# A planner that follows all DMA transfers as a fluid, without hand-set nudges, and with a new order of loads

## The chip, the cores and the metric

The kernel runs on one core of one Trainium2 chip. The metric is device time in microseconds (us), lower is better. "Span" is the time from the first to the last instruction in one profiled execution; the device time of the same execution is some 1.8 us longer. Runs that are compared were made on the same chip in one sitting, the kernel before among them each time. Slow executions are left out of every ratio; a single execution has no known state.

## The reference

Windowed attention with a few global keys and a linear distance bias, then a two-layer block with the activation h - tanh(h):

```python
# q, k, v: (4 batches, 8 heads, 768 positions, 64), n_global = 8, n_local = 96
scores = scale * np.matmul(q, k.transpose(0, 1, 3, 2))
...
keep = is_global | is_local
bias = -slopes[:, None, None] * dist[None, :, :]
scores = np.where(keep, scores + bias, -1e9)
a = softmax(scores)                                  # cut: max, exp, sum written out
attn_out = np.matmul(a, v)

x = attn_out.transpose(0, 2, 1, 3).reshape(B * S, H * D)   # (3072, 512)
h = x @ w_in                                         # (512, 2048)
g = h - np.tanh(h)
return g @ w_out                                     # (2048, 512)
```

## The kernel before

The 3072 rows are 24 query tiles of 128. Each tile goes: load q, k, v (GpSimd); transpose q and k (on TensorE for tiles 0 to 5, by a DMA from SyncE from tile 6 on); scores (TensorE); exponential (ScalarE); mask (DVE); attention times v (TensorE); normalize (DVE); transpose x (TensorE, from tile 9 on a DMA from SyncE); the first product `m1` (TensorE); tanh (ScalarE); h - tanh(h) (DVE, called `g`); the second product `m2` (TensorE); eviction (ScalarE or DVE); store (issued by ScalarE). The operations that matter below:

```python
def a_DT(u):                                  # transpose of q and k, one DMA
    qk[u] = kpool.tile([P, 2, NP, P], BF16, name="qk")
    nc.sync.dma_start_transpose(out=..., in_=kq.pop(u)...)          # cut

def m1_th(g, f0):                             # ScalarE, PSUM -> "th", 3 buffers
    nc.scalar.activation(h_view(ths[g, f0], g, m), h_view(hs[g, f0], g, m), AF.Tanh, bias=0.0, scale=1.0)

def m1_g(g, f0):                              # DVE, frees the PSUM bank of m1
    nc.vector.tensor_tensor(out=gs[b][:, f0 : f0 + m, o : o + n], in0=h_view(hs.pop((g, f0)), g, m),
                            in1=h_view(ths.pop((g, f0)), g, m), op=ALU.subtract)

def store(u, part):
    lo, hi = parts(u)[part]
    eng = nc.sync if u == NU - 1 else nc.scalar
    eng.dma_start(out=out[SEQ[u] * P : (SEQ[u] + 1) * P, lo:hi], in_=ots[u][:, lo:hi])
```

The order on each engine isn't written by hand. A planner simulates the engines when the program is built: again and again it takes the operation that can start first, with its own estimate of durations, buffers, PSUM banks and DMA landings. The instructions are then emitted in the order of planned start. An engine executes them strictly in that order.

```python
op(("st", u, part), SP if u == NU - 1 else ACT, ..., lambda ...: store(u, part), after=[("ev", u, part)],
   give=["ot"] if part == len(parts(u)) - 1 else [], dma=T_ST)
...
NUDGE = { ('AV', 21): -0.3, ('E', 12, 1): 0.3, ... ('m2', 2, 1): 1.0, ... }   # 58 entries; cut
...
ring = {SP: [0.0, []], POOL: [5.8, []]}       # two DMA queues; ScalarE's stores count as SP
...
    via = POOL if o["eng"] is POOL else SP
    if o["dma"] and len(ring[via][1]) >= 8:   # at most eight in flight
        t = max(t, sorted(ring[via][1])[-8])
    ...
    c = (round(t + NUDGE.get(key, 0.0), 3), o["pri"], n)      # the least c goes next
...
order, model_end = plan()
with tc.manual_schedule(engines={PE, ACT, DVE, POOL, SP}):
    ...
    for t, key in with_warm(order):
        ops[key]["fn"]()
```

The softmax here doesn't subtract the row's maximum and nothing guards it: scores larger than these inputs give would overflow.

## Time and profile before

| | before |
|---|---|
| device time, median of the first 3 runs (lowest to highest) | 214.13 us (213.65 to 215.67) |
| span of the profiled execution | 212.3 us |
| TensorE busy | 203.8 us, 96% |
| granted TensorE clock | 1.0 in the mean |
| stalls of TensorE after the start | 1.21 us at 55.6 us, 0.73 us at 71.8 us |

The prediction below shows the lines of the profile and builds an account from them, with the terms "work ahead" and "lag".

How to read the lines: a timeline row has start, duration, engine, source line, operation, tiles, shapes, count, and in square brackets the idle time before it with what ended that. "ACTq" and "SPq" are the DMA issues of ScalarE and SyncE. A row of a waits view has the engine that waited, what it waited for, the total in us, the number of times, and the longest.

### The profile page before, as it was taken

What the parts mean: (1) busy time and instruction counts of PE and PEld (TensorE: products, weight loads), DVE (VectorE), ACT (ScalarE), POOL (GpSimd) and SP (SyncE); (2) the same over time, 40 slices, a digit from 0 to 9 for tenths busy, and PEclk for the clock granted to TensorE, in tenths of its full rate; (3) what the DMA queues carried; (4) which work ended last, traced back from release to release, by engine and by line L of the source; (5) the groups of instructions that cost most, each with busy time, mean ns of one, the idle gap of its engine ahead of it and who ended that gap; (6) DMA issues with size and microseconds to landing.
All of it is one profiled execution on the core that took longest, in us unless ns stands there. A gap on an engine that the chain in (4) does not pass through costs nothing.

```text
span 212.3 us, 5296 instructions
## 1 busy us (share of the span) xinstructions
PE 203.8 (96%) x2172; PEld 145.4 (68%) x2198; DVE 132.1 (62%) x269; ACT 120.4 (57%) x184; POOL 71.9 (34%) x92
## 2 busy tenths in 40 slices
PE   7899999999799899999999999999999999999994
PEld 2679995984466767577677578757755786666754
DVE  6579796656475777385667487757655594343611
ACT  4777865553446786487358465667545773444410
POOL 8995676667344365345342700000000000000000
PEclk9999999999999999999999999999999999999999
DMA  5999999999999999999999999212362220110112
GB/s 181 182 189 177 180 203 180 187 157 167 159 158 186 151 137 181 144 181 184 153 169 164 165 142 193 50 74 53 99 112 90 77 49 0 52 51 16 37 49 100
DMA packets 106073, 27.49 MB, mean 129 GB/s; under 512 B 94656, under 2 KB 103104, under 8 KB 106048
## 3 DMA queue, kind: packets, MB, share of 16 engines
q0 software_dynamic: 74048, 13.11, 84.9%
q1 hardware_dynamic: 28144, 7.48, 26.6%
q10 hardware_dynamic: 3856, 6.56, 9.7%
q8 instruction: 17, 0.28, 0.6%
q14 instruction: 8, 0.07, 0.1%
HBM read 27.26 MB, written 6.29 MB: 158 GB/s over the span
## 4 chain that ended last, share of the span: by engine, by line
PE 82%; DMA 13%; DVE 1%; issue 1%; POOL 0%; ACT 0%; SPq 0%; DVEq 0%
PE ps L410 38%; PE ps L444 32%; DMA qk<-kq 6%; DMA kq<-in_q_dram 5%; PE ps L314 5%; PE ps L342 2%; DMA kf<-in_k_dram 2%; PE ps L346 2%; PE ps L277 1%; PE ps L281 1%; PE ps L369 1%; PE ps L165 1%; POOL kq L242 0%; DVE kh L296 0%; DVE g L429 0%
## 5 line engine op out<-in xcount | busy, mean ns | idle before, releaser
L410 PE MATMUL ps<-xT,w_in_bf 128*128 128x256 bf16 (+1 forms) x960 | 93.0, 251 | 0.1
L444 PE MATMUL ps<-w_out_bf,g 128*128 128x512 bf16 (+3 forms) x391 | 87.3, 362 | 1.6 <-issue 0.5
L410 PEld LDWEIGHTS <-w_in_bf 128*128 128x128 bf16 x960 | 77.5, 98 | 13.3 <-DMA w_in_bf<-in_moe_w_in_dram 0.3
L429 DVE TENSOR_TENSOR g<-ps,th 128x512 bf16<-128x512 f32 (+1 forms) x102 | 64.9, 656 | 28.5 <-ACT th L422 27.8
L422 ACT ACTIVATE th<-ps 128x512 f32<-128x512 f32 (+1 forms) x102 | 56.8, 573 | 38.1 <-PE ps L410 35.0
L444 PEld LDWEIGHTS <-g 128*128 128x128 bf16 x416 | 37.9, 98 | 33.7
L323 ACT ACTIVATE pd<-ps 128x1024 bf16<-128x1024 f32 x24 | 24.4, 1024 | 14.0 <-PE ps L314 14.0
L236 POOL DMA_DIRECT2D vb<-in_v_dram x24 | 21.4, 894 | 14.3 <-DMA kq<-in_k_dram 4.6
L242 POOL DMA_DIRECT2D kq<-in_k_dram x20 | 17.7, 886 | 23.6 <-DMA qk<-kq 16.4
L323 ACT ACTIVATE po<-ps 128x1024 bf16<-128x1024 f32 x20 | 20.2, 1023 | 6.1 <-PE ps L314 6.1
L242 POOL DMA_DIRECT2D kq<-in_q_dram x20 | 17.7, 886 | 7.8 <-DMA vb<-in_v_dram 7.6
L329 DVE TENSOR_TENSOR pd<-pd,mk 128x1024 bf16<-128x1024 bf16 x20 | 13.8, 690 | 6.2 <-ACT pd L323 6.2
L355 DVE TENSOR_TENSOR x<-ps,rden 128x512 bf16<-128x512 f32 x24 | 16.6, 692 | 0.8
L454 ACT COPY ot<-ps 128x512 f32<-128x512 f32 x16 | 9.4, 585 | 13.7 <-PE ps L444 13.7
L329 DVE TENSOR_TENSOR po<-po,mk 128x1024 bf16<-128x1024 bf16 x20 | 13.7, 687 | 2.7 <-ACT po L323 2.7
L342 PE MATMUL ps<-vb,pd 128*128 128x65 bf16 x192 | 14.1, 193 | 0.0
L342 PEld LDWEIGHTS <-pd 128*128 128x128 bf16 x192 | 12.5, 98 | 1.4 <-issue 0.2
L454 DVE COPY ot<-ps 128x512 f32<-128x512 f32 (+3 forms) x10 | 5.8, 585 | 12.0 <-PE ps L444 11.9
L314 PEld LDWEIGHTS <-qk 64*128 64x128 bf16 x288 | 8.1, 94 | 7.0 <-issue 4.0
L314 PE MATMUL ps<-qk 64*128 64x128 bf16 x288 | 10.8, 217 | 1.9 <-DMA qk<-kq 1.9
L346 PE MATMUL ps<-vb,po 128*128 128x65 bf16 x160 | 12.4, 193 | 0.0
L346 PEld LDWEIGHTS <-po 128*128 128x128 bf16 x160 | 10.4, 97 | 1.1
(48 smaller groups left out, 81.9 us busy)
## 6 DMA issues: line engine op xcount, KB each, us to landing
out_dram<-ot ACTq DMA_DIRECT2D x23, 256.0 KB, 6.1
vb<-in_v_dram POOLq DMA_DIRECT2D x24, 128.0 KB, 10.9
kq<-in_k_dram POOLq DMA_DIRECT2D x22, 128.0 KB, 11.2
kq<-in_q_dram POOLq DMA_DIRECT2D x22, 128.0 KB, 11.2
w_in_bf<-in_moe_w_in_dram POOLq DMA_DIRECT2D x8, 256.0 KB, 8.3
w_out_bf<-in_moe_w_out_dram POOLq DMA_DIRECT2D x8, 256.0 KB, 8.7
kf<-in_k_dram SPq DMA_DIRECT2D x2, 256.0 KB, 4.5
qf<-in_q_dram ACTq DMA_DIRECT2D x2, 256.0 KB, 3.7
```

The costliest lines, as they stand in the source:

```text
L236: i = nc.gpsimd.dma_start(out=v_of(u)[:, :, 0:Dh], in_=by_head)
L242: i = nc.gpsimd.dma_start(out=dst.rearrange("p (h d) -> p h d", d=Dh), in_=by_head)
L314: nc.tensor.matmul(s[:, slot(2 * p + hh), :], kT(prev_of[u] if o else u)[r, p, :], qk[u][r, 0, p, :], start=u >= B, stop=True, skip_group_ ...
L323: nc.scalar.activation(pr[u, o].rearrange("q (a h) f -> q a h f", a=2)[:, part], sc[u, o][:, part, :].rearrange("q a (h f) -> q a h f", f= ...
L329: nc.vector.tensor_tensor(out=pr[u, o], in0=pr[u, o], in1=mk[:, :, mask_of(u, o) - 1, :], op=ALU.mult)
L342: nc.tensor.matmul(dst, pr[u, 0][:, slot(h), :], v_of(u)[:, h, :], start=True, stop=last,)
L346: nc.tensor.matmul(dst, pr[u, 1][:, slot(h), :], v_of(prev_of[u])[:, h, :], start=False, stop=True,)
L355: nc.vector.tensor_tensor(out=xs[u].rearrange("q (a h) d -> q a h d", a=2), in0=t[:, :, :, 0:Dh], in1=rden.to_broadcast([P, 2, H // 2, Dh] ...
L410: nc.tensor.matmul(t[:, (f - f0) * n : (f - f0 + 1) * n], w_in_bf[j][:, c, fo : fo + P], xT[b][:, c, o : o + n], start=(c == 0), stop=(c = ...
L422: nc.scalar.activation(h_view(ths[g, f0], g, m), h_view(hs[g, f0], g, m), AF.Tanh, bias=0.0, scale=1.0)
L429: nc.vector.tensor_tensor(out=gs[b][:, f0 : f0 + m, o : o + n], in0=h_view(hs.pop((g, f0)), g, m), in1=h_view(ths.pop((g, f0)), g, m), op= ...
L444: nc.tensor.matmul(os_[u, part][:, 0 : hi - lo], gs[b][:, f, t * P : (t + 1) * P], w_out_bf[f // FJ][:, f % FJ, lo:hi], start=(f == 0), st ...
```

## The change

The intent: replace 58 hand-set nudges and a rough model of two DMA queues by a better model. GpSimd, SyncE and ScalarE have a queue each, the queues share the DMA engines at rates that depend on which of them are active, and every issue makes the planner estimate all landings in flight anew. With a better estimate, the safety margin on a transpose's landing falls from 4 us to 1 us. The order of loads is new too.

```diff
-    NUDGE = {
-        ('AV', 21): -0.3,
... (56 more)
-        ('th', 9, 8): 0.15,
-    }
-    SLACK_DT, SLACK_DX = 4.0, 4.0
+    NUDGE = {}
+    SLACK_DT, SLACK_DX = 1.0, 1.0
-    T_ROWS, T_LD, T_W, T_ST, T_DT, T_DX = 0.67, 0.89, 1.3, 0.7, 1.75, 0.9
-    LOADS = "ttttiiitiiiotoooioitooo"
+    T_ROWS, T_LD, T_W, T_ST, T_DT, T_DX = 0.67, 0.89, 1.3, 0.65, 1.05, 0.55
+    RING = 5.8
+    TAIL = {POOL: 0.45, SP: 0.8, ACT: 0.8}
+    SHARE = { (True, False, False): (1.0, 0, 0), ... (True, True, True): (0.3, 0.29, 0.2) }   (cut)
+    LOADS = "ttttiiiitiiootooiiotooo"
...
-        ring = {SP: [0.0, []], POOL: [5.8, []]}
-        share = {SP: 0.5, POOL: 0.5}
+        flying, landed, at_dma = {POOL: [], SP: [], ACT: []}, {POOL: [], SP: [], ACT: []}, [0.0]
+        def fly(jobs, t, t_end): ...        (the fluid; cut)
+        def fly_from(q, key, t, end): ...   (an issue: all landings anew; cut)
...
-                via = POOL if o["eng"] is POOL else SP
-                if o["dma"] and len(ring[via][1]) >= 8:
-                    t = max(t, sorted(ring[via][1])[-8])
+                if o["dma"] and len(landed[eng]) >= 8:
+                    t = max(t, done[landed[eng][-8]])
```

Only the planner changes; the same operations are executed in another order (the planner may give a copy to ScalarE or to DVE). The last lines: before, a transfer of SyncE or ScalarE waits for the eighth before it of both together; after, for the eighth before it of its own engine.

More of the change, by code (lines that the diff above doesn't have):

```diff
@@ L466 @@
     INF = 1.0e9
-    NUDGE = {
-        ('AV', 21): -0.3,
-        ('E', 12, 1): 0.3,
-        ('E', 13, 0): 0.3,
-        ('E', 13, 1): -0.6,
-        ('E', 14, 1): -0.6,
-        ('E', 17, 0): -0.15,
-        ('E', 17, 1): -0.15,
-        ('E', 18, 1): 0.15,
-        ('E', 21, 1): 1.0,
-        ('E', 9, 1): -0.3,
-        ('M', 14, 1): 0.3,
-        ('M', 20, 0): 1.0,
-        ('M', 9, 1): 1.0,
-        ('R', 15): 0.6,
-        ('R', 9): -0.3,
-        ('S', 3, 0): 0.15,
-        ('S', 6, 0): 1.0,
-        ('S', 7, 0): 0.6,
-        ('V', 16): -0.15,
-        ('V', 19): -0.6,
-        ('V', 4): -0.3,
-        ('X', 6): 0.15,
-        ('Xe', 9): -0.3,
-        ('ev', 7, 0): 1.0,
-        ('g', 1, 6): 0.3,
-        ('g', 11, 6): 0.6,
-        ('g', 13, 14): 0.3,
-        ('g', 2, 2): 0.6,
-        ('g', 7, 14): 1.0,
-        ('g', 7, 8): 0.6,
-        ('g', 9, 2): 1.0,
-        ('m1', 12, 0): 0.6,
-        ('m1', 4, 4): -0.3,
-        ('m1', 4, 8): -0.15,
-        ('m1', 5, 0): -0.3,
-        ('m1', 5, 4): -0.3,
-        ('m1', 5, 8): -0.15,
-        ('m1', 6, 2): 0.6,
-        ('m1', 8, 6): 1.0,
-        ('m1', 9, 8): 0.6,
-        ('m2', 1, 2): 1.0,
-        ('m2', 10, 0): 1.0,
-        ('m2', 11, 0): -0.3,
-        ('m2', 12, 3): 0.3,
-        ('m2', 15, 1): 0.3,
-        ('m2', 2, 1): 1.0,
-        ('m2', 21, 1): 0.6,
-        ('m2', 3, 0): 0.6,
-        ('m2', 3, 2): 1.0,
-        ('m2', 5, 3): 1.0,
-        ('m2', 7, 1): 0.3,
-        ('m2', 7, 3): 0.3,
-        ('m2', 8, 0): 1.0,
-        ('st', 12, 0): 0.6,
-        ('st', 8, 0): 1.0,
-        ('th', 6, 10): -0.6,
-        ('th', 7, 10): 0.3,
-        ('th', 9, 8): 0.15,
-    }
-    SLACK_DT, SLACK_DX = 4.0, 4.0
+    NUDGE = {}
+    SLACK_DT, SLACK_DX = 1.0, 1.0
     WARM = (1.1, 7.0)
@@ L530 @@
     FETCH = (15.8, 0.9)
-    T_ROWS, T_LD, T_W, T_ST, T_DT, T_DX = 0.67, 0.89, 1.3, 0.7, 1.75, 0.9
-    LOADS = "ttttiiitiiiotoooioitooo"
+    T_ROWS, T_LD, T_W, T_ST, T_DT, T_DX = 0.67, 0.89, 1.3, 0.65, 1.05, 0.55
+    RING = 5.8
+    TAIL = {POOL: 0.45, SP: 0.8, ACT: 0.8}
+    SHARE = {
+        (True, False, False): (1.0, 0, 0), (False, True, False): (0, 1.0, 0), (False, False, True): (0, 0, 1.0),
+        (True, True, False): (0.36, 0.42, 0), (True, False, True): (0.5, 0, 0.42), (False, True, True): (0, 0.5, 0.42),
+        (True, True, True): (0.3, 0.29, 0.2),
+    }
+    LOADS = "ttttiiiitiiootooiiotooo"
     first, n_of = [], {"t": 0, "i": 0, "o": 0}
@@ L722, in find, with fly @@
             return at, got
-        ring = {SP: [0.0, []], POOL: [5.8, []]}
-        share = {SP: 0.5, POOL: 0.5}
         done, start, width = {}, {}, {}
+        flying, landed, at_dma = {POOL: [], SP: [], ACT: []}, {POOL: [], SP: [], ACT: []}, [0.0]
+        def fly(jobs, t, t_end):
+            fin = {}
+            while t < t_end:
+                if FETCH[0] <= t < FETCH[0] + FETCH[1]:
+                    t = min(FETCH[0] + FETCH[1], t_end)
+                    continue
+                heads = [q for q in jobs if jobs[q] and jobs[q][0][1] <= t]
+                later = min([jobs[q][0][1] for q in jobs if jobs[q] and jobs[q][0][1] > t] + [t_end])
+                if not heads:
+                    t = later
+                    continue
+                rate = SHARE[tuple(q in heads for q in (POOL, SP, ACT))]
+                rate = {q: r for q, r in zip((POOL, SP, ACT), rate)}
+                dt = min([later - t] + [jobs[q][0][2] / rate[q] for q in heads])
+                if t < FETCH[0]:
+                    dt = min(dt, FETCH[0] - t)
+                t += dt
+                for q in heads:
+                    jobs[q][0][2] -= dt * rate[q]
+                    if jobs[q][0][2] < 1e-6:
+                        key = jobs[q].pop(0)[0]
+                        fin[key] = t + TAIL[q] + ops[key]["slack"]
+            return fin
@@ new lines, in fly_from @@
+        def fly_from(q, key, t, end):
+            busy = flying[POOL] and q is SP and key[0] != "st"
+            done.update(fly(flying, at_dma[0], t))
+            at_dma[0] = max(at_dma[0], t)
+            begin = end + (2.0 if q is POOL else 1.0)
+            if key[0] in ("T", "Xe"):
+                begin = t + (4.2 if busy else 2.2)
+            if q is POOL:
+                begin = max(begin, RING)
+            flying[q].append([key, begin, ops[key]["dma"], q])
+            landed[q].append(key)
+            done.update(fly({k: [list(j) for j in v] for k, v in flying.items()}, at_dma[0], INF))
@@ L727, in plan, with due_at, at_of @@
+        flies = {key: any(a[0] != "issue" and ops[a]["dma"] for a in o["after"]) for key, o in ops.items()}
+        def due_at(key):
+            if flies[key] or key not in since:
+                since[key] = max(
+                    [0.0] + [start[a[1]] if a[0] == "issue" else done[a] for a in ops[key]["after"]]
+                )
+            return since[key]
+        def at_of(x):
+            return done[x] if isinstance(x, tuple) else x
         f1 = f2 = 0.0
@@ L758, in plan @@
             for key in ready:
-                if key not in since:
-                    since[key] = max([0.0] + [start[a[1]] if a[0] == "issue" else done[a] for a in ops[key]["after"]])
                 if key[0] == "S" and len(ops[key]["hold"]) > 2:
-                    due = min(due, since[key] + YIELD)
+                    due = min(due, due_at(key) + YIELD)
             for key, n in cand:
@@ L768, in plan @@
                 t = free[eng]
-                via = POOL if o["eng"] is POOL else SP
-                if o["dma"] and len(ring[via][1]) >= 8:
-                    t = max(t, sorted(ring[via][1])[-8])
-                if key not in since:
-                    since[key] = max([0.0] + [start[a[1]] if a[0] == "issue" else done[a] for a in o["after"]])
-                t = max(t, since[key])
+                if o["dma"] and len(landed[eng]) >= 8:
+                    t = max(t, done[landed[eng][-8]])
+                t = max(t, due_at(key))
                 if key[0] == "m1" and t >= due:
@@ L788, in plan @@
                         break
-                    t = max(t, sorted(avail[p])[n_p - 1])
+                    t = max(t, sorted(at_of(x) for x in avail[p])[n_p - 1])
                 if t is None:
@@ L807, in plan @@
             elif o["dma"]:
-                via = POOL if o["eng"] is POOL else SP
-                mine, other, part = ring[via], ring[SP if via is POOL else POOL], share[via]
-                begin = max(mine[0], end + (1.0 if via is SP else 1.97))
-                both = min(max(0.0, other[0] - begin), o["dma"] / part)
-                mine[0] = begin + o["dma"] + both * (1 - part)
-                if begin < FETCH[0] <= mine[0]:
-                    mine[0] += FETCH[1]
-                other[0] += both * part
-                done[key] = mine[0] + (0.8 if via is SP else 0.45) + o["slack"]
-                mine[1].append(done[key])
+                fly_from(o["eng"], key, t, end)
             else:
@@ L834, in plan @@
             for p in o["take"]:
-                avail[p].remove(min(avail[p]))
+                avail[p].remove(min(avail[p], key=at_of))
             for p in o["give"]:
-                avail[p].append(done[key])
+                avail[p].append(key if o["dma"] and not o["at"] else done[key])
             order.append((t, key))
```

## The prediction

> **What bounds the kernel now.** I read the page from the top: busy time per engine, then the DMA queues, then the chain of work that ended last, and after that the waits of TensorE and single stretches of its timeline.
>
> ```profile
> span 212.3 us, 5296 instructions
> PE 203.8 (96%) x2172; PEld 145.4 (68%) x2198; DVE 132.1 (62%) x269; ACT 120.4 (57%) x184; POOL 71.9 (34%) x92
> ...
> q0 software_dynamic: 74048, 13.11, 84.9%
> q1 hardware_dynamic: 28144, 7.48, 26.6%
> q10 hardware_dynamic: 3856, 6.56, 9.7%
> ...
> PE 82%; DMA 13%; DVE 1%; issue 1%; POOL 0%; ACT 0%; SPq 0%; DVEq 0%
> ```
>
> TensorE is busy 96% of the span and carries 82% of the chain; a DMA carries 13% of it. The loads from GpSimd (q0) and the transposes from SyncE (q1) fill the DMA engines until about 130 us. Next, who made TensorE wait at all (wait in total, times, longest):
>
> ```profile
> PE ps L392 <- DVE zero L874: 1.0, 1, 1.0
> PE ps L277 <- DVE kq L255: 0.5, 1, 0.5
> PE ps L314 <- DMA qk<-kq: 1.9, 2, 1.2
> ```
>
> Only the last of these lies after the start, and its two waits stand in the timeline of TensorE at 55.62 and 71.78 us:
>
> ```profile
> 55.62 0.62 PE L314 MATMUL ps<-qk 64*128 64x128 bf16 x16 [1.21 <-DMA qk<-kq]
> 71.78 0.62 PE L314 MATMUL ps<-qk 64*128 64x128 bf16 x16 [0.73 <-DMA qk<-kq]
> ```
>
> They are the score matmuls of query tiles 7 and 10, waiting for DMA transposes of q and k. Between these stalls TensorE is dense. I added up the work that stands ahead of each operation in TensorE's order, with durations from the chain of this trace: eight matmuls of 256 columns 0.87 us, four of 512 columns 0.86, sixty-four of 128 columns 3.57, twenty-four score matmuls 0.78 plus about 0.1 to refill behind them, sixteen attention-times-v matmuls 0.5, four transposes 0.22. All work is 200.6 us. Call "lag" the start in the trace less the work ahead. The lag is 6.7 to 6.9 us from 18 to 54 us, 8.1 after the first stall, 8.8 after the second, and still 8.8 at the last score matmuls at 165 us. So the whole run is 200.6 + 8.8 + about 2.9 for the last eviction and stores = 212.3. In that account the time can change only by the start, by stalls, and by the last stores. The lag at the end is simply the largest "landing less work ahead" among all data that TensorE needs.
>
> **What the Trainium skill says.** "TensorE: Matmul & The Clock Gate", section "Wait — 56ns, not 53.3ns?", gives 55.6 ns from start to start for 128 columns when warm and 215.7 for 512. This trace agrees: 3.57/64 = 55.8 ns and 0.86/4 = 215 ns. So the dense stretches have nothing left to give. "Perfetto Trace Analysis", section "Identifying the Most-Contended Engine", warns that matmul busy time is no measure of the distance to the best possible; here that is why I use the work sum and not the 96%. "DMA: Bandwidth & Descriptors", section "Issuing engines are not separate DMA queues", says that transfers from SyncE, ScalarE and GpSimd run on the same 16 engines and interleave. The trace agrees: the store issued at 52.1 us took 7.5 us to land beside loads and transposes, the one at 137.7 us took 2.0 alone. The same page's "Queues, rings and completion order" has each ring consumed in order; the 33 transposes of SyncE here landed in the order of their issue.
>
> **The change part by part.** No operation is added or removed: each engine has the same instructions (4398 rows on TensorE in both) and the same 200.6 us of work. Changed are the planner's model of DMA (three queues that share the engines; store and transpose costs lower; safety margin on transposes 4 us down to 1), the 58 hand-set nudges (gone), and the load order. What follows is order alone.
>
> Load order: input weight block 3 goes ahead of tile 4, output block 1 ahead of tile 5, input block 7 ahead of output block 4. In the GpSimd queue a weight block takes about 1.3 us between landings and a tile load 0.8 to 1.0. Block 3 then lands at about 17.9 + 1.3 = 19.2 us (it was 21.2), output block 1 at 26.4 (was 29.0), tile 4's k at 19.95 (was 18.65). The new TensorE order uses them at once: the matmuls on block 3 stand behind 12.25 us of work (was 15.16), the first output matmuls behind 20.1 (was 25.5). With the lag at 7.0 these want their data at 19.25 and 27.1: just met. The matmuls on input block 2 come 0.2 us sooner in the work (10.91, was 11.12) but the block lands at 17.91 either way, and they already waited for it. So the lag after the start is about 7.0 instead of 6.75: +0.25 us, nothing removed.
>
> Stores: the outputs of tiles 1 and 2 finish after 38.4 and 40.2 us of work, so their stores go out near 47 and 50.5 us instead of 52.1 and 56.3. About one store (256 KB) more is then in flight before the transpose of tile 7 lands. q10's share, 9.7% of 212.3 us, is 20.6 us for 23 stores and two loads: 0.8 us each. Tile 7's transpose, issued at 45.9 and landing at 55.55, can slip by up to 0.8.
>
> Score matmuls, landing as in the trace against the new work ahead:
> tile 7: 55.55 to 56.4, work 48.58 (was 47.52): lag 7.0 to 7.8.
> tile 8: 58.76 and up to 0.5 more, work 51.85: 6.9 to 7.4.
> tile 9: 63.5, work 58.30: 5.2.
> tile 10: 71.73, work 64.67 (was 62.92): 7.1.
> tile 11: 74.6, work 67.93 (was 69.29): 6.7.
> tiles 12 and 13 (one run of three blocks): 86.8, work 77.38 (was 79.11): 9.4.
> all later runs: lag needed below 8.3, since their transposes land 5 us or more ahead of use before, and move by at most 4.4 us of work.
>
> So both old stalls (1.21 and 0.73) go away, and a new one appears at the run that needs tile 13. Its data, from the transfers' own view:
>
> ```profile
> L285 SPq DMA_TRANSPOSE qk<-kq x1: 2255/2255/2255, 76.7 to 76.7; - x1
> ...
> DMA to landing us min/median/max: 10.1/10.1/10.1
> ...
> 87.96 0.84 PE L314 MATMUL ps<-qk 64*128 64x128 bf16 x24
> ```
>
> 76.7 + 10.1 = 86.8; before, TensorE came to it at 87.96 and had 1.1 us to spare. Now it comes at 77.38 + 7.6 = 85.0, the lag of 7.6 being the tile 7 stall, or the x transpose for tile 9, which now queues behind tile 12's transpose (from 78.8 to about 81.5, work ahead of its user 73.89). It waits about 1.8 us. The sum in lag: start +0.25, old stalls −1.95, stalls at tile 7, 8 or 9 about +0.6, stall at tile 13 about +1.8: near +0.6 us in all.
>
> **The rivals.** (a) The planner's fluid picture is right and tile 13's transpose really lands sooner, because stores 1 and 2 and the x transpose are spread otherwise; then the lag ends at about 7.6, 1.2 us under the present one: 212.9. For it: the planner has been fitted to more queues. Against it: tile 13's q load (issued at 60.85, 15.7 us to landing) came in at 76.57, only 0.1 us before the transpose was issued, and the DMA share is at or over 1.5 in every stretch from 45 to 95 us, so the engines have no idle time in which to bring it forward; the same bytes stand ahead of it. (b) Stores and transposes collide worse: the thinner margin leaves stalls at several runs, and tile 13 slips with the store of tile 6 (out near 82 us instead of 85). Each slip of a microsecond there goes straight into the end: 216 to 217. (c) ScalarE and DVE become the bound without the nudges: the gap between a tile's scores and its attention matmuls is 3.3 us at the tightest (tiles 7 and 8) against 2 × 1.02 for the exponentials and 0.69 for the mask, plus latencies: about 3.0. The kernel before ran without a wait at 3.5. This is worth 0.1 to 0.5 us in all. (d) The new load order starves the start: each of the just-met landings could cost a few tenths, but a lag of up to 9.4 is swallowed by tile 13 anyway.
>
> **Range and chances.** Tile 13 as before gives 214.1 + 0.6 = 214.7; rival (a), at about one in four, 212.9; rival (b) 216. I take 214.4 us, and 212.8 to 216.3 for 8 in 10. Faster by over 2% (below 209.9) would need a lag of 4.6, less than the start alone takes: 1%. Slower by over 2% (above 218.4) needs over 4 us of new stalls: 4%. Within 2%: 95%.
>
> **What would show it.** The waits of TensorE should have no stall over 0.2 us at tile 10, one up to about 0.8 near 55.6 us or none, and one of 1 to 2.5 us before a run of 24 score matmuls near 85 us; TensorE's busy time unchanged; stores of tiles 1 and 2 issued 5 us sooner; after 90 us the timeline dense to the end. I am wrong if that run finds its data landed (then rival a), if the largest stall is elsewhere, or if the end comes with waits on ScalarE or DVE.

## The result and the profile after

| | before | after |
|---|---|---|
| median of 4 runs (lowest to highest) | 214.42 us (213.65 to 215.67) | 221.49 us (221.09 to 221.8) |
| span | 212.3 us | 220.0 us |
| granted clock, mean | 1.0 | 0.984 |

The ratio is 1.032 (95% interval 1.027 to 1.038), slower. A ratio here is the mean time of one kernel's fast runs over that of the other's of the same rounds, so it isn't quite the ratio of the medians. The prediction of 214.4 us (212.8 to 216.3) missed by 7 us.

From the page of the kernel after: span, busy time, the granted clock in 40 slices of 5.5 us (9 is 90% or more), the queue of GpSimd's loads, and the chain that ended last.

```profile
span 220.0 us, 5306 instructions
PE 206.6 (94%) x2169; PEld 146.8 (67%) x2198; DVE 129.3 (59%) x269; ACT 119.9 (55%) x184; POOL 71.9 (33%) x92
...
PEclk9999999999679999999999999999999999999999
...
q0 software_dynamic: 74048, 13.11, 83.7%
...
PE 85%; DMA 8%; POOL 4%; DVE 1%; issue 1%; ACTq 0%; ACT 0%
```

Neither DMA nor ScalarE nor DVE is busier than before, and the clock falls in slices 11 and 12, from 55 to 66 us, which it did not before. So one place is to be looked at. The waits of TensorE confirm it:

```profile
PE ps L410 <- DVE g L429: 6.7, 1, 6.7
PE ps L392 <- DVE zero L857: 1.0, 1, 1.0
```

One stall of 6.7 us, and neither of the two old ones. The first product waits for `g` on DVE because `g` is what frees its PSUM banks. The three timelines side by side, first ScalarE of the kernel after:

```profile
48.66 1.02 ACT L323 ACTIVATE po<-ps 128x1024 bf16<-128x1024 f32 x1
57.01 0.34 ACTq L459 DMA_DIRECT2D out_dram<-ot  x1
57.40 1.08 ACT L422 ACTIVATE th<-ps 128x512 f32<-128x512 f32 x2 [7.72 <-DMA qk<-kq]
```

Then DVE:

```profile
49.71 0.69 DVE L329 TENSOR_TENSOR po<-po,mk 128x1024 bf16<-128x1024 bf16 x1 [0.22 <-ACT po L323]
58.02 1.29 DVE L429 TENSOR_TENSOR g<-ps,th 128x512 bf16<-128x512 f32 x2 [7.62 <-ACT th L422]
```

Then TensorE:

```profile
58.77 1.86 PE L410 MATMUL ps<-xT,w_in_bf 128*128 128x128 bf16 x16 [6.75 <-DVE g L429]
```

ScalarE stood still for 7.7 us, DVE behind it for 7.6, TensorE behind that for 6.75. What ended ScalarE's wait is named a DMA transpose of q and k, which a tanh doesn't read. The row between explains it: the first thing ScalarE did at 57.01 was to *issue a store*. A tanh that was ready stood in line behind it. The chain of waits through this stretch says the same in order of time (start, duration, what):

```profile
43.85 0.89 PE ps L410 x16
44.75 0.88 PE ps L444 x4
...
46.76 10.18 DMA qk<-kq
...
57.01 0.34 ACTq L459
57.35 0.05 issue
57.40 0.61 ACT th L422
58.00 0.02 issue
58.02 0.70 DVE g L429
58.73 0.04 issue
58.77 1.86 PE ps L410 x16
60.63 1.71 PE ps L444 x4
```

The transpose that starts at 46.76 is tile 7's; it landed at 56.93. The store that went out 0.08 us later is the output of tile 2. It has nothing to do with tile 7. The chain also shows the second cost: sixteen matmuls of 128 columns took 0.89 us before the stall and 1.86 us after it, four of 512 columns 0.88 and 1.71. TensorE came back at half speed.

In lag: 7.0 us up to the stall, 16.15 at the scores of tile 7, level at 16.1 up to tile 13's scores. Of the rise of 9.1 us, 6.75 is the stall and 9.1 - 6.75 = 2.4 the cold clock. At the last matmul the lag is 15.9 us, against 8.7 before: 7.2 us. The end behind it was about 0.4 us longer; with rounding, that makes up the difference in span of 7.7.

**Why the store waited for tile 7.** The built program's list of instructions has the semaphores that each instruction waits for. In the kernel after, ScalarE (the first number counts rows of the listing; a wait-only instruction is merged into the row that follows it):

```
36 L459 DMACopy out_dram<-ot 128x512 [waits DMAHW3_49,DVE_49]
37 L422 Activation th<-ps 128x512 [waits PE_49]
38 L323 Activation pd<-ps 128x1024 [waits PE_49]
39 L323 Activation po<-ps 128x1024 [waits PE_49]
40 L459 DMACopy out_dram<-ot 128x512 [waits DMAHW5_49,DVE_49]
41 L422 Activation th<-ps 128x512 [waits PE_49]
```

and the first weight load of tile 7's scores on TensorE:

```
1405 L314 Ldweights qk [waits DMAHW5_49]
```

Both wait for the semaphore DMAHW5: it is the completion semaphore of tile 7's transpose, and the store is about to use it for itself, so it first waits until the earlier user is done. Transfers of SyncE and ScalarE together take eight such semaphores in turn. The turn is in the order in which the built program places them, not in the order of time: the transposes of tiles 6 to 11 take theirs ahead of every store. In this table T is a transpose, st a store, and each line is the turn:

```
before: ld ld ld ld T6 T7 T8 T9 T10 T11 st0 st1     st2 st3 st4 ...   st2 takes that of T6, st3 of T7, st4 of T8
after:  ld ld ld ld T6 T7 T8 T9 T10 T11 st0 st1 T12 st2 st3 st4 ...   st2 takes that of T7, st3 of T8, st4 of T9
```

The transpose T12 moved ahead of st2, and the store of tile 2 is planned earlier (after 43.5 us of TensorE's work, it was 51.0). In the kernel before st2 went out at 56.34, 11 us after T6 had landed (45.07), and it stood behind an exponential, in ScalarE's timeline of the kernel before:

```profile
56.06 1.02 ACT L323 ACTIVATE pd<-ps 128x1024 bf16<-128x1024 f32 x1 [1.02 <-PE ps L314]
56.34 0.34 ACTq L459 DMA_DIRECT2D out_dram<-ot  x1
56.98 1.02 ACT L323 ACTIVATE po<-ps 128x1024 bf16<-128x1024 f32 x1
```

The Trainium skill, "Perfetto Trace Analysis", section "DMA Instruction — HWDGE (DVE, Sync)", puts the wait for semaphores in the sequencer, ahead of the profiled start of a DMA instruction. The trace agrees: the store's row says 0.34 us and starts 0.08 us after the earlier user of its semaphore had landed, and the wait turns up as idle time before the tanh.

### The profile page after: what moved, and what is told of

It is laid out like the page before. It is cut to its first block, busy times and chain, and to the rows that moved or that the text cites. A ratio compares the mean times of both kernels' runs of the same rounds, so it can differ in the third digit from the quotient of the medians.

```text
span 220.0 us, 5306 instructions
## 1 busy us (share of the span) xinstructions
PE 206.6 (94%) x2169; PEld 146.8 (67%) x2198; DVE 129.3 (59%) x269; ACT 119.9 (55%) x184; POOL 71.9 (33%) x92
## 4 chain that ended last, share of the span: by engine, by line
PE 85%; DMA 8%; POOL 4%; DVE 1%; issue 1%; ACTq 0%; ACT 0%
PE ps L410 38%; PE ps L444 36%; DMA qk<-kq 5%; PE ps L314 5%; DMA w_in_bf<-in_moe_w_in_dram 3%; PE ps L342 2%; PE ps L346 2%; POOL vb L236 2%; POOL kq L240 1%; PE ps L369 1%; DVE ot L454 0%; PE ps L277 0%; POOL w_in_bf L249 0%; DVE g L429 0%; ACTq L459 0%
## 5 line engine op out<-in xcount | busy, mean ns | idle before, releaser
L410 PE MATMUL ps<-xT,w_in_bf 128*128 128x256 bf16 (+1 forms) x960 | 97.7, 253 | 7.0 <-DVE g L429 6.7
L410 PEld LDWEIGHTS <-w_in_bf 128*128 128x128 bf16 x960 | 78.3, 99 | 24.4 <-issue 6.8
L444 PE MATMUL ps<-w_out_bf,g 128*128 128x512 bf16 (+3 forms) x388 | 90.4, 364 | 1.4
L454 ACT COPY ot<-ps 128x512 f32<-128x512 f32 x17 | 10.0, 585 | 16.0 <-PE ps L444 16.0
L454 DVE COPY ot<-ps 128x512 f32<-128x512 f32 (+3 forms) x9 | 5.2, 573 | 10.8 <-PE ps L444 10.8
```

Of the source, the lines that this page charges most:

```text
L410: nc.tensor.matmul(t[:, (f - f0) * n : (f - f0 + 1) * n], w_in_bf[j][:, c, fo : fo + P], xT[b][:, c, o : o + n], start=(c == 0), stop=(c = ...
L444: nc.tensor.matmul(os_[u, part][:, 0 : hi - lo], gs[b][:, f, t * P : (t + 1) * P], w_out_bf[f // FJ][:, f % FJ, lo:hi], start=(f == 0), st ...
```

## The experiments

My theory at this point: (T) the whole loss is this one store, blocked on ScalarE until tile 7's transpose lands, plus the cold clock behind it; everything else in the prediction holds. Rivals: (R1) ScalarE's and DVE's order without the nudges is worse altogether, and the loss would stay or appear elsewhere; (R2) the store waits for something about itself (its data, the DMA engines being full), not for the semaphore's earlier user; (R3) the new load order or the thinner margins make tile 7's transpose late. In the expectations T is called theory S, R1 and R2 are rival D, and R3 is part of rival F (the fluid planner or the load order is what costs).

### One store moved later on ScalarE

The kernel after, with the plan left alone but one entry moved:

```diff
 order, model_end = plan()
+at_plan = {key: t for t, key in order}
+MOVED = {('st', 2, 0): at_plan[('E', 7, 1)] + 0.001}
+order = sorted(((MOVED.get(key, t), key) for t, key in order), key=lambda x: x[0])
```

> The changed kernel with one thing moved: the store of tile 2 is issued on ScalarE after the exponentials of tile 7 instead of before the tanh of tile 4's last block. No other order changes. Theory S (the shared landing semaphore): ScalarE's 7.3 us wait in front of that store was for the landing of tile 7's transpose, whose semaphore the store takes over; everything ScalarE had behind it starved TensorE. Then the idle time of 6.75 us near 52 us and the slow clock after it are gone, the lag of TensorE near 50 to 65 us is 7 to 8 and not 16, and the time is 213 to 216 us: up to 214.7 if tile 13's transpose lands at 86.8 as I took it (lag 9.4), near 213 if it lands sooner. Rival D (the DMA engines are congested by earlier stores and loads, or ScalarE is slower without nudges): a stall of several us stays between 50 and 60 us and the time stays above 219.

Measured: 215.25 us (213.27 to 216.74, 4 runs, one of them slow), ratio 1.0008 (0.990 to 1.012), span 212.6, granted clock 1.0. The built program shows the store still waiting for DMAHW5, but now behind the exponentials of tile 7, which need the same transpose anyway. It went out at 56.28 (tile 7's transpose landed at 55.56) and held up nobody. The next two stores still left 0.08 us after the landings of tiles 8 and 9 (58.45 after 58.37, 63.98 after 63.90); these short waits didn't reach TensorE. The whole 7 us are gone with one store, and R1 falls. In TensorE's timeline what is left is this:

```profile
81.64 2.78 PE L410 MATMUL ps<-xT,w_in_bf 128*128 128x256 bf16 x24 [0.70 <-DMA xT<-x]
```

This is a wait for the x transpose of tile 9, which the prediction had put at about 81.5 and which landed at 81.60. Tile 13's transpose landed at 86.24 (predicted 86.8) and cost 0.45 us. So with the store out of the way the prediction's own table of landings held.

### The store of tile 1 in two halves

One more transfer in turn ahead of the store of tile 2, so that it takes the semaphore of tile 8's transpose and not tile 7's. The data, the bytes and the plan are the same.

```diff
-        eng.dma_start(out=..., in_=ots[u][:, lo:hi])
+        for lo, hi in ((0, 256), (256, 512)) if u == 1 else ((lo, hi),):
+            eng.dma_start(out=..., in_=ots[u][:, lo:hi])
```

> The changed kernel with the store of tile 1 issued as two halves. That puts one more transfer between tile 7's transpose and the store of tile 2, so that the eighth transfer before that store is now tile 8's transpose. Theory S: ScalarE waits at the store of tile 2 until the transpose of tile 8 lands (59.9 us in the changed kernel), 3 us longer: TensorE's idle time near 52 us grows from 6.75 to 9.5 to 10 us, and the time from 221.5 to 224 to 225. Rival D: no change over 0.5 us, since the bytes are the same.

Measured, one run (so its state is unknown, and the trace carries the argument): 223.19 us, span 221.4. The store waited for DMAHW6, tile 8's transpose, which landed at 59.03. ScalarE:

```profile
59.10 0.34 ACTq L460 DMA_DIRECT2D out_dram<-ot  x1
59.49 1.09 ACT L422 ACTIVATE th<-ps 128x512 f32<-128x512 f32 x2 [9.72 <-DMA qk<-kq]
```

TensorE's stall grew from 6.75 to 9.04 us. The wait moves with the semaphore to the landing of a transfer that neither the store nor the tanh reads: R2 falls.

### The kernel before without its nudges; the kernel after with the old load order

```diff
(first, from the kernel before)             (second, from the kernel after)
-    NUDGE = { ... 58 entries }             -    LOADS = "ttttiiiitiiootooiiotooo"
+    NUDGE = {}                             +    LOADS = "ttttiiitiiiotoooioitooo"
```

> The kernel before with its 58 nudges taken out and nothing else (old planner, old load order). The planner then puts the store of tile 2 at 43.5 us of TensorE's work, as in the changed kernel, and the eighth transfer before it is again tile 7's transpose. Theory S: the same stall appears without the fluid planner and without the new loads: ScalarE waits from about 50 to 55.6 us, TensorE idles 4 to 6 us there, and the time is 218 to 222. If the fluid planner or the load order is what costs (rival F), this kernel is within 2 us of the kernel before, 213 to 216.

> The changed kernel with the old order of loads. The store of tile 2 is again put early (42.6 us of work) and again takes the semaphore of tile 7's transpose. Theory S: the stall stays, within 1.5 us of the changed kernel: 220 to 223. Rival F in its form 'the load order costs': back to 213 to 216.

Measured: without nudges 221.70 us (2 runs), ratio 1.034 (1.026 to 1.041); with old loads 221.26 us (2 runs), ratio 1.032 (1.023 to 1.040). With two runs each, the record calls both "unclear" against the 2% mark; the traces settle what the times leave open. Both have the same wait at the same place. ScalarE in the kernel before without nudges:

```profile
56.49 0.34 ACTq L459 DMA_DIRECT2D out_dram<-ot  x1
56.88 1.08 ACT L422 ACTIVATE th<-ps 128x512 f32<-128x512 f32 x2 [7.49 <-DMA qk<-kq]
```

Tile 7's transpose landed at 56.42 there, and TensorE stalled for 6.51 us. So the old planner, with the old loads and the old margins, puts the store in the same place once its nudges are gone. Neither the fluid model nor the load order nor the thin margins are needed for the loss: R3 falls. The nudges had, without anybody saying so, kept a store off a semaphore.

### One nudge in, one nudge out

In plans made without each of the 58 nudges in turn, a single one decides whether the store of tile 2 goes early: `('m2', 2, 1): 1.0`. I put it alone into the kernel after, and took it alone out of the kernel before.

> The changed kernel with one nudge, 1.0 on the second quarter of tile 2's output matmuls. The store of tile 2 then comes late (51.9 us of work), but the store of tile 3 comes early (44.4) and takes over the semaphore of tile 8's transpose, which lands near 59 us. Theory S: ScalarE waits at the store of tile 3 from about 51 to 59 us, 8 us; TensorE idles 7 to 9 us there and the time is 221.5 to 224. If it is something about the store of tile 2 itself or about the outputs of tiles 1 and 2 (rival), the stall is gone and the time is 213 to 216.

> The kernel before with one of its 58 nudges taken out (the second quarter of tile 2's output matmuls, 1.0). The store of tile 2 moves from 51.0 to 43.8 us of work and then takes over the semaphore of tile 7's transpose (before: tile 6's). Theory S: ScalarE waits at it from about 50 to 55.6 us; the exponentials of tile 6 are behind it, so the attention matmuls of tile 6 start near 59.0 instead of 54.5: lag 11.4, time 216 to 218. Rival (nudges matter only in the sum): within 1 us of the kernel before.

Both missed on size. One nudge in: 218.05 us, one run. I had reckoned that the store of tile 2 would take tile 8's semaphore; but the turn goes by position, and with the nudge tile 3's store came third. It took tile 7's semaphore and left at 54.99, 0.07 us after the landing at 54.92:

```profile
54.99 0.34 ACTq L459 DMA_DIRECT2D out_dram<-ot  x1
55.38 1.08 ACT L422 ACTIVATE th<-ps 128x512 f32<-128x512 f32 x2 [5.76 <-DMA qk<-kq]
```

TensorE's stall was 3.89 us. One nudge out: 225.51 us, one run, the worst of all. The store of tile 2 now came second, so that the third in turn was tile 1's. Three stores in a row, at 54.99, 64.33 and 69.42, left 0.07 us after the landings of the transposes of tiles 7, 9 and 10. The second of them cost the most; ScalarE and then TensorE:

```profile
64.33 0.34 ACTq L459 DMA_DIRECT2D out_dram<-ot  x1
64.77 1.02 ACT L323 ACTIVATE pd<-ps 128x1024 bf16<-128x1024 f32 x1 [6.24 <-DMA qk<-kq]
```

```profile
65.84 3.09 PE L444 MATMUL ps<-w_out_bf,g 128*128 128x512 bf16 x8 [3.12 <-ACT pd L323]
```

I had counted the wait of one store and not those of the next two. The blocked stores are the same mechanism in both runs, and both expectations went wrong in part because I still thought of a certain tile's store and not of its place in the turn. But blocked stores aren't the whole of the 225.51 us. TensorE ran at half speed for 3.41 us from 66.37. Later, where no store was held, it waited again for the masks (1.40 and 0.71 us) and for the x transpose of tile 9 (1.06 us, landed at 94.53), and it ran at half speed for 6.83 us from 93.67. Whether the blocked stores brought this second part about is not shown.

### The kernel before with the new load order

> The kernel before with the new order of loads only. The store of tile 2 takes over tile 6's semaphore, as in the kernel before: no wait of ScalarE over 2 us at a store. But the score matmuls of tile 10 stand behind 60.3 us of work and tile 13's behind 75.7: with the landings of the kernel before (71.7 and 86.8) the lag is 11.1 to 11.4, 2.4 us more than before: 216 to 217.5. If only the store matters, 214 to 215.

Measured: 221.59 us (2 runs), ratio 1.032 (1.026 to 1.037), clock 1.0. A miss, and another cause. No store is held up to the landing of a semaphore's earlier user; TensorE waits for data instead:

```profile
PE ps L314 <- DMA qk<-kq: 4.1, 3, 2.4
PE ps L410 <- DMA xT<-x: 3.4, 2, 2.3
```

The transposes of tiles 8 and 9 landed at 61.94 and 65.98 (58.76 and 63.48 before), though the one of tile 8 was issued at the same time (48.5), and those of x then at 80.81 and later. It is a second way to lose 7 us, without the first. That the nudges are fitted to one order of loads would explain it, but this is argued and not shown. Why tile 8's transpose took 13.4 us in place of 10.2 isn't settled. The first three stores went out at 46.8, 51.9 and 54.9, so that up to three were in flight beside it, which may be it; no run tells that apart.

### One line in the planner, and then a second store moved

The lesson as a planner rule: the store of tile 2 may not be planned before tile 7's transpose has landed.

```diff
-   lambda u=u, part=part: store(u, part), after=[("ev", u, part)],
+   lambda u=u, part=part: store(u, part), after=[("ev", u, part), ("T", 7) if u == 2 else None],
```

> The changed kernel with one line more in the planner: the store of tile 2 may be planned only after tile 7's transpose has landed. Everything is planned anew from there. Theory S: the long wait is gone. With the landings of the run with the store moved late, the largest lag that TensorE needs is 7.9 us (tile 7 at 55.6 less 47.7 of work; tile 13 needs only 7.2, the x transpose of tile 9 about 5.7), against 8.85 in the kernel before: span 200.6 + 7.9 + 2.9 + about 0.1 = 211.5, time 213.3, a ratio to the kernel before of 0.993 to 0.998. If other waits of stores behave the same way elsewhere (rival D), the time is above 216.

Measured: 215.83 us (6 runs), ratio 1.005 (1.002 to 1.009), span 213.2. The 6.75 us stall is gone, but I missed by over 2 us on the time. TensorE had the tile 7 stall (0.96 us) and one more, and ScalarE shows where that came from; TensorE first:

```profile
66.68 1.03 PE L410 MATMUL ps<-xT,w_in_bf 128*128 128x256 bf16 x8 [1.05 <-DVE g L429]
```

```profile
64.86 0.34 ACTq L459 DMA_DIRECT2D out_dram<-ot  x1
65.30 1.08 ACT L422 ACTIVATE th<-ps 128x512 f32<-128x512 f32 x2 [1.84 <-PE ps L346]
```

That is the store of tile 4, behind the landing of tile 9's transpose (64.79) by 0.07 us. The row of the tanh names TensorE as what ended the idle time, which misleads: the tanh began when the store was out (64.86 + 0.34 and 0.1 between). So in a second step I moved this store too, behind the exponentials of tile 9:

```diff
+at_plan = {key: t for t, key in order}
+MOVED = {('st', 4, 0): at_plan[('E', 9, 1)] + 0.001}
+order = sorted(((MOVED.get(key, t), key) for t, key in order), key=lambda x: x[0])
```

> The kernel of the run with the planner line for the store of tile 2, with one thing more: the store of tile 4 is moved on ScalarE behind the second exponentials of tile 9, so that it no longer stands ahead of a tanh while tile 9's transpose is in flight. My theory (a store's issue blocks ScalarE until the transfer whose semaphore it takes has landed, and that is all that is left over): the tile 7 stall of about 1.0 us stays, the 1.05 us stall at 66.7 us goes, the lag ends near 8.1 us in place of 9.1, the span is 212.0 to 212.4 and the time 213.4 to 214.1, which is 0.995 to 0.998 of the kernel before. Rival (the stall at 66.7 us is the planner's own misjudgement of tanh and g): it stays, and the time stays at 215 to 216.

Measured: 215.96 us (6 runs), ratio 1.005 (0.9998 to 1.011), span 214.0. Half right. The stall at 66.7 us went, as the theory said. But the time didn't move, for TensorE now waits for two transposes:

```profile
56.07 0.62 PE L314 MATMUL ps<-qk 64*128 64x128 bf16 x16 [1.50 <-DMA qk<-kq]
76.62 0.62 PE L314 MATMUL ps<-qk 64*128 64x128 bf16 x16 [1.16 <-DMA qk<-kq]
```

Tile 7's transpose landed at 56.02 (55.49 in the run before). The two programs' orders differ only behind that, so half a microsecond there lies between two executions (on two chips) and not in the edit. Tile 11's landed at 76.58 (75.77), and TensorE, no longer held back by the store, came to it 1.2 us too early. This is the prediction's picture again: the lag at the end is the largest "landing less work ahead", and taking away a smaller one uncovers the next. No version here beats the kernel before beyond the noise. The three without the long wait come out at 1.001 to 1.005 of it; the one with the planner line alone is 0.2 to 0.9% slower, clear of the noise.

## Why the prediction was wrong, by its own steps

- *The order of loads and the start*: right. Input block 3 landed at 18.82 us (19.2 predicted), output block 1 at 26.57 (26.4), tile 4's k at 19.75 (19.95). The lag behind the start was 7.0.
- *The old stalls at tiles 7 and 10 go away*: right by the letter, but for another reason. In the kernel after a lag of 16 us swallows them. With the one store moved they came out as said: 0.16 us at tile 7, none at tile 10.
- *Stores*: this is the step that failed. The prediction said: "the outputs of tiles 1 and 2 finish after 38.4 and 40.2 us of work, so their stores go out near 47 and 50.5 us". The first went out at 46.37. The second went out at 57.01. The step took a store to leave when its data is ready, and counted it only as 256 KB more in flight, worth up to 0.8 us for tile 7. What the runs showed in its place: a store's issue also waits for the last user of its completion semaphore, it waits *on ScalarE*, and everything behind it in ScalarE's order waits with it. The term that was missing is 6.75 us of stall and 2.4 us of cold clock.
- *Rival (c)*, ScalarE or DVE as the bound: it looked at the right engine, but reckoned with durations (exponentials, mask) alone, at 0.1 to 0.5 us. ScalarE was busy 55% of the time in the kernel after. What counted was not how much it does but what stands first in its line. Two signs that the prediction had named for being wrong came true: the largest stall was elsewhere, and TensorE waited on DVE, behind ScalarE.
- *Tile 13 as the place of the new stall, and the x transpose of tile 9*: not seen in the kernel after, again swallowed. With the store moved, both were there: 0.70 us at 81.64 and 0.45 us at 86.29. They cost 1.15 us together; predicted were 1.8 for tile 13 alone, had nothing stalled ahead of it.
- *The chances*: 4% for slower by over 2% rested on the sentence "No operation is added or removed ... What follows is order alone". Order alone is where a wait can hide. (The four copies that changed between ScalarE and DVE make "each engine has the same instructions" not quite exact; no run puts a cost on them.) The program's list of instructions with their waits was to be had before the run, and showed `DMAHW5` at the store; I read it for order and not for waits.
- *The clock* wasn't in the account at all. The Trainium skill, "TensorE: Matmul & The Clock Gate", section "What's actually happening", gives half speed after an idle window of about 3.4 us. The trace agrees for the long stall: after 6.75 us of idle time the same sixteen matmuls took 1.86 us in place of 0.89, and the granted clock was 0.5 from 56.40 to 63.22. So this stall cost a third more than itself. The window is no safe bound, though: in the run with one nudge out, half speed came after 3.12 us of idle time, and once more after waits of at most 1.40 us, with TensorE busy for 0.53 and 1.14 us in the 3.41 us before. The stalls of 2.40 us and less in the kernel before with the new loads left the clock at 1.0.

## What to carry to other kernels

A DMA issue stands in an engine's line like any other instruction, and it waits there for its data *and* for the completion semaphore that it reuses; on an engine with other work, look up whose semaphore that is before moving the issue. When a plan is re-ordered, list for each transfer the earlier user of its semaphore and when that lands; stores belong behind work that needs the same landing anyway. Idle time that is put down to data which the waiting instruction doesn't read is the sign of such a wait.

## What the Trainium skill lacked or had wrong

- "DMA: Bandwidth & Descriptors", section "Issuing engines are not separate DMA queues", says that issuing from several engines "will only save the time on the sequencer it takes to initiate the DMA, which is usually small". It lacks the warning that the issue can hold up its engine's other work (that a semaphore is waited for on the issuing sequencer does stand elsewhere on that page, without a size): here ScalarE stood still for 7.7 us ahead of an issue whose own row says 0.34 us, and for 9.7 us in the run with the split store.
- No page found says that in a built program the transfers of SyncE and ScalarE share eight completion semaphores in turn, in the order of the program and not of time. More than a dozen stores left within 0.02 to 0.08 us after the landing of an unrelated transpose (56.93 and 57.01 for tile 2's; 58.50 and 58.57, 64.79 and 64.86 in the run with the planner line).
- "TensorE: Matmul & The Clock Gate", section "What's actually happening", gives the cold clock after at least one idle window of about 3.4 us. In the run with one nudge out it came after 3.12 us of idle time, and after a stretch of 3.41 us in which TensorE was busy for 1.14 us; a stretch of the same length with 1.63 us busy (from 98.30 in the kernel before with the new loads) left the clock at 1.0. Where the bound lies isn't shown.
